# Query expansion in 32x64 tiles, numerators of all heads in one bank, and kv formed without a turn

One Trainium2 chip, one core. The metric is the device time of one execution in microseconds (us); lower is better. "Filled stretch" means the time from 25 us to about 255 us, in which TensorE never waits; "the head" is what comes before it. A turn is a transpose on TensorE, and a dummy is a product of zeros that only keeps TensorE busy.

## The reference

Attention with sketched features, then a feed-forward block with exact gelu:

```python
# q, k, v: (4 batches, 4 heads, 1088 tokens, 32);  S1, S2: (8, 32)
def phi(x):                                   # 64 features from two factors of 8
    a = einsum('rd,bhsd->bhsr', S1, x); b = einsum('rd,bhsd->bhsr', S2, x)
    return outer(a, b)                        # i, j -> 64
q_p, k_p = phi(q), phi(k)
kv  = einsum('bhsf,bhsd->bhfd', k_p, v)       # 64 x 32 per head
z   = k_p.sum(tokens)                         # 64 per head
x   = (q_p @ kv) / (q_p @ z + 1e-6)           # -> (4352, 128)
out = gelu(x @ w_in) @ w_out                  # w_in 128 x 2048, w_out 2048 x 128
```

The products are in fp32. The sketches and the feed-forward weights arrive in 64 bits and are first rounded to fp32 in steps named low words, fields, exponents, mantissas and signs. Each matrix product in the kernel is run by TensorE as two passes, each with its own weight load; the counts in the profile are passes (the 4 products of an expansion stand as x8).

## The kernel before: what the change and the argument touch

Heads are h = 2c + r: pair c, parity r. F = 64 features, D = 32, J = 8 blocks of 128 tokens; the 64 tokens a batch that are left are the rest tokens. `lhsT` is the stationary operand (the weight), `rhs` the moving one. A product takes a tile of the array, given as rows x columns; a change to another shape is a change of mode. I take it that the partitions of the output pick the column tile; the starts in the traces below bear this out (pairs 7 ns apart with outputs at two places, 58 ns apart at one).

```python
def kv_product(ps, lhsT, rhs, h, at, start=False):      # kv^T: v is the weight (32 columns)
    r = h % 2
    pe.matmul(ps[at * D:(at + 1) * D, r * F:(r + 1) * F], lhsT=lhsT, rhs=rhs, start=start, stop=False, ...)

def kv_first(ps, r):                                    # batch 0; v_aug = v | ones, 64 columns
    for i in range(J):
        ch, t, one = i // 4, i // 2 % 2, i % 2
        for c in range(NP):
            pe.matmul(ps[c * F:(c + 1) * F, r * F:(r + 1) * F], lhsT=v_aug[r][:, c, i, :],
                      rhs=k_p[0, r][:, t, c * 4 + ch * 2 + one].rearrange("p i j -> p (i j)"), ...)

def kv_sum(b, ps):                                      # batches 1 to 3
    for i in range(J):
        for h in range(H):
            kv_product(ps, main["v", b][:, h, i, :], k_p[b, h % 2][...], h, h, start=i == 0)
    # [cut] column sums of the features against ones, for z

def turn_kv(b, ps, copy):                               # kv^T -> kv, then the copy that attention reads
    # [cut] one transpose (b == 0) or two products with the identity
    copy(out=kz[b].rearrange("p c n -> p (c n)"), in_=ps[:, :128])

def expand_products(n):                                 # both factors of q: 4 products, 32 x 128 tiles
    for g in range(4):
        rows = slice(g * D, (g + 1) * D)
        pe.matmul(B_of[n][g // 2][:, g % 2, :W], lhsT=Srep[rows]..., rhs=qT[n][rows]..., start=True, stop=True)

def attend(n, ...):                                     # 4 products, 64 x 64 tiles, one bank per parity
    for c in range(NP):
        for r in range(2):
            pe.matmul(banks[r][c * F:(c + 1) * F, c0:c1], lhsT=kz[b][r * F:(r + 1) * F, c, :],
                      rhs=qp[n][r * F:(r + 1) * F, c, c0:c1], start=True, stop=True)
    # [cut] 4 copies of denominators on ScalarE, reciprocal, 4 multiplications on VectorE
```

## Time and profile before

| | before |
|---|---|
| time, median | 272.4 us (272.14 to 272.43) |
| span of the profiled run | 270.3 us |
| TensorE busy, share of the chain of waits | 98%, 95% |
| VectorE / ScalarE / GpSimd busy | 62% / 54% / 63% |
| first hidden product starts | 16.53 us |

The lines stand in the prediction below. One view of before that it leaves out is needed later: the chain in order of time (start us, duration us, engine, line, passes), where the first batch's kv is formed:

```profile
8.69 1.08 PE o_ps L414 x32
...
10.13 1.08 PE o_ps L414 x32
11.21 0.38 PE o_ps L434 x8
```

32 passes take 1.08 us, twice (L414), and the rest tokens 0.38 (L434).

### The profile page before, as it was taken

To read this page: it belongs to the slowest core of one execution; us is meant where nothing else is said; L and a number is where in the kernel's file an instruction comes from. 1 tells how busy PE (TensorE), PEld (TensorE's weight loads), DVE (VectorE), ACT (ScalarE), POOL (GpSimd) and SP (SyncE) were. 2 spreads that over 40 slices of the span, in tenths; PEclk is the share of its full clock that TensorE was granted. 3 is DMA by queue.
4 is the path that set the end of the run, shared out by engine and by line. 5 is a ranking of instruction groups with operands and counts; after the bars stand their busy time and mean duration, and the time that the engine had idled before them with its cause. 6 is when DMAs were issued, how large, how long until landed. Compare 5 with 4: busy or idle time off the path is not lost.

```text
span 270.3 us, 5814 instructions
## 1 busy us (share of the span) xinstructions
PE 264.2 (98%) x2320; PEld 135.7 (50%) x2320; DVE 167.4 (62%) x263; ACT 145.8 (54%) x291; POOL 171.5 (63%) x178
## 2 busy tenths in 40 slices
PE   7999999999999999999999999999999999999994
PEld 5735445354445545435445445444544544445794
DVE  6896888534795699679225997487048902750140
ACT  4784777566645633673367433763367334733431
POOL 3431007899998499368865897568856886777300
PEclk9999999999999999999999999999999999999999
DMA  6569263635201100110200000100200020011020
GB/s 198 171 172 359 54 170 65 171 75 143 53 2 21 21 0 2 21 22 0 42 0 2 0 0 12 32 0 4 38 0 2 1 39 4 1 22 19 2 39 20
DMA packets 37915, 13.50 MB, mean 50 GB/s; under 512 B 28288, under 2 KB 37248, under 8 KB 37888
## 3 DMA queue, kind: packets, MB, share of 16 engines
q1 hardware_dynamic: 37648, 13.05, 19.2%
q8 instruction: 18, 0.29, 0.5%
q10 hardware_dynamic: 240, 0.08, 0.1%
q14 instruction: 9, 0.07, 0.1%
HBM read 10.90 MB, written 2.23 MB: 49 GB/s over the span
## 4 chain that ended last, share of the span: by engine, by line
PE 95%; DVE 2%; DMA 1%; issue 0%; ACT 0%; ACTq 0%; DVEq 0%
PE h_ps L576 44%; PE o_ps L653 32%; PE o_ps L704 5%; PE w_ps L471 3%; PE w_ps L701 3%; PE w_ps L516 2%; PE w_ps L405 1%; PE w_ps L354 1%; DMA raw_SR<-in_S_dram 1%; PE o_ps L414 1%; PE h_ps L542 0%; PE w_ps L434 0%; DVE bits_m L272 0%; PE w_ps L542 0%; PE o_ps L310 0%
## 5 line engine op out<-in xcount | busy, mean ns | idle before, releaser
L576 PE MATMUL h_ps<-xT,w_in 128*64 128x512 f32 (+3 forms) x518 | 140.8, 577 | 0.2 <-DVE xT L561 0.2
L583 ACT ACTIVATE block<-h_ps 128x512 f32<-128x512 f32 (+1 forms) x128 | 72.8, 570 | 95.5 <-PE h_ps L576 93.1
L653 PE MATMUL o_ps<-block,w_out 128*64 128x256 f32 x224 | 57.8, 380 | 0.0
L576 PEld LDWEIGHTS h_ps<-xT,w_in 128*64 128x64 f32 (+1 forms) x518 | 42.1, 143 | 30.3 <-issue 10.1
L618 POOL TENSOR_TENSOR bits_low<-block 128x512 f32<-128x512 f32 x28 | 36.6, 1308 | 25.9 <-ACT block L583 25.7
L653 PEld LDWEIGHTS o_ps<-block,w_out 128*64 128x64 f32 x224 | 30.0, 137 | 38.4 <-issue 29.6
L619 POOL TENSOR_TENSOR bits_a<-block 128x512 f32<-128x512 f32 x28 | 36.9, 1316 | 16.2 <-ACT block L583 16.1
L492 DVE TENSOR_TENSOR q_pT<-A_sb,w_ps 64x512 f32<-64x512 f32 x32 | 22.1, 690 | 32.6 <-ACT A_sb L478 31.9
L621 POOL TENSOR_TENSOR bits_m<-block,bits_e 128x512 f32<-128x512 f32 x28 | 36.3, 1295 | 2.2
L620 POOL TENSOR_TENSOR bits_e<-bits_a,block 128x512 f32<-128x512 f32 x28 | 36.1, 1290 | 2.2
L524 DVE RECIPROCAL den<-den 128x512 f32<-128x512 f32 (+1 forms) x7 | 21.9, 3122 | 12.6 <-ACT den L523 12.6
L653 PE MATMUL o_ps<-bits_a,small 128*64 128x256 f32 x112 | 29.0, 382 | 0.0
L653 PE MATMUL o_ps<-bits_m,w_out 128*64 128x256 f32 x112 | 28.7, 379 | 0.0
L653 PE MATMUL o_ps<-block,small 128*64 128x256 f32 x112 | 28.7, 379 | 0.0
L653 PE MATMUL o_ps<-bits_low,small 128*64 128x256 f32 x112 | 28.7, 379 | 0.0
L653 PEld LDWEIGHTS o_ps<-block,small 128*64 128x64 f32 x112 | 15.3, 137 | 18.0 <-issue 12.8
L669 DVE TENSOR_TENSOR sums<-o_ps,sums 64x512 f32<-64x512 f32 x8 | 5.5, 682 | 24.6 <-ACT sums L666 24.6
L478 ACT COPY A_sb<-w_ps 64x512 f32<-64x512 f32 (+1 forms) x36 | 17.7, 557 | 3.9 <-PE w_ps L471 3.8
L528 DVE TENSOR_TENSOR xT<-w_ps,den 32x512 f32<-32x512 f32 (+1 forms) x28 | 18.2, 648 | 1.0
L653 PE MATMUL o_ps<-bits_e,small 128*64 128x256 f32 x112 | 16.8, 379 | 0.0
L704 PE MATMUL o_ps<-g,w_out 128*128 128x512 f32 x32 | 16.4, 599 | 0.3 <-ACT xT L561 0.3
L523 ACT ACTIVATE den<-w_ps 32x512 f32<-32x512 f32 (+1 forms) x28 | 15.6, 558 | 1.3 <-PE w_ps L516 1.0
(158 smaller groups left out, 320.4 us busy)
## 6 DMA issues: line engine op xcount, KB each, us to landing
block<-in_moe_w_in_dram SPq DMA_DIRECT2D x3, 512.0 KB, 7.2
block<-in_moe_w_out_dram SPq DMA_DIRECT2D x3, 512.0 KB, 9.9
k<-in_k_dram SPq DMA_DIRECT2D x48, 32.0 KB, 1.9
v<-in_v_dram SPq DMA_DIRECT2D x3, 512.0 KB, 4.2
q<-in_q_dram SPq DMA_DIRECT2D x24, 64.0 KB, 3.6
out_dram<-oT SPq DMA_DIRECT2D x24, 64.0 KB, 2.2
k<-in_k_dram SPq DMA_DIRECT2D x2, 256.0 KB, 3.1
q<-in_q_dram SPq DMA_DIRECT2D x2, 256.0 KB, 4.2
```

Source lines behind the costliest of these rows:

```text
L478: act.copy(out=A[g // 2][F:, g % 2, :width[n]], in_=B_of[n][g // 2][:F, g % 2, :width[n]])
L492: dve.tensor_mul(out=cols[r * F:(r + 1) * F], in0=a[:, :, r::2], in1=b[:, :, r::2])
L524: dve.reciprocal(out=den[:, :W], in_=den[:, :W])
L528: dve.tensor_mul(out=xT[n][rows, :W], in0=banks[h % 2][rows, :W], in1=den[rows, :W])
L576: pe.matmul(ps[rows, :W], lhsT=w[:, rows], rhs=xT[n][:, :W], start=True, stop=True)
L583: act.activation(out=g_of[n, fi][:, :W], in_=ps[:, :W], func=ACT.Gelu)
L618: pool.tensor_sub(out=s[3], in0=a11, in1=a21)
L619: pool.tensor_add(out=s[1], in0=a21, in1=a22)
L620: pool.tensor_sub(out=s[2], in0=s[1], in1=a11)
L621: pool.tensor_sub(out=s[4], in0=a12, in1=s[2])
L653: pe.matmul(acc[n][bank][half * 64:(half + 1) * 64, col:col + HW], lhsT=fixed, rhs=moving, start=opens and e == 0 and name in "4715", stop ...
L704: pe.matmul(o_of[n], lhsT=w_tile(w_out_sb, fi), rhs=g, start=first, stop=final)
```

## The change

Three parts. (1) kv is formed directly: the features become the weight, v moves, so no turn is needed. (2) The query expansion puts both factors of a head on the same partitions: 16 products in 32x64 tiles in place of 4 in 32x128; half the copies and multiplications follow. (3) The attention puts the numerators of all heads in one bank: 8 products in 64x32 tiles, then one multiplication. Also two small dummy products in the head, one older dummy ahead of the token attention dropped, and some rounding of weights moved between engines there. The zeros of the dummies shrink to one column, so that the first warm-up product starts at 0.93 us and not at 1.20.

```diff
-    def kv_product(ps, lhsT, rhs, h, at, start=False):
-        r = h % 2
-        pe.matmul(ps[at * D:(at + 1) * D, r * F:(r + 1) * F], lhsT=lhsT, rhs=rhs, start=start, ...)
+    def kv_product(ps, features, rhs, h, at, start=False):
+        c, r = h // 2, h % 2
+        pe.matmul(ps[r * F:(r + 1) * F, c * 2 * D + at:c * 2 * D + at + rhs.shape[1]],
+                  lhsT=features..., rhs=rhs, start=start and c == 0, ...)
     def kv_first(ps, r):
         for i in range(J):
             for c in range(NP):
-                pe.matmul(ps[c * F:(c + 1) * F, r * F:(r + 1) * F], lhsT=v_aug[r][:, c, i, :], rhs=k_p[0, r][...], ...)
+                kv_product(ps, k_p[0, r][...], v_aug[r][:, c, i, :], 2 * c + r, 0, start=i == 0)
     def kv_sum(b, ps):
-                kv_product(ps, main["v", b][:, h, i, :], k_p[b, h % 2][...], h, h, start=i == 0)
+                kv_product(ps, k_p[b, h % 2][...], main["v", b][:, h, i, :], h, h % 2 * D, start=i == 0)
-    def turn_kv(b, ps, copy):   [cut]
     def expand_products(n):
-        for g in range(4):
-            pe.matmul(B_of[n][g // 2][:, g % 2, :W], lhsT=Srep[rows]..., rhs=qT[n][rows]..., ...)
+        for s in range(2):
+            for g in range(G):
+                for r in range(2):
+                    pe.matmul(B_of[n][g // 2][r * F:(r + 1) * F, g % 2, s * W // 2:(s + 1) * W // 2],
+                              lhsT=Srep[rows, s]..., rhs=qT[n][rows, r::2]..., ...)
     def attend(n, ...):
-                    pe.matmul(banks[r][c * F:(c + 1) * F, c0:c1], lhsT=kz[b][r * F:(r + 1) * F, c, :], ...)
+                    for part, ps in ((r, over), (1 - r, under)):
+                        pe.matmul(ps[c * F + part * D:c * F + (part + 1) * D, c0:c1],
+                                  lhsT=kz[b][r * F:(r + 1) * F, c, part * D:(part + 1) * D], ...)
-        for h in range(H):
-            dve.tensor_mul(out=xT[n][rows, :W], in0=banks[h % 2][rows, :W], in1=den[rows, :W])
+        dve.tensor_mul(out=xT[n][:, :W], in0=over[:, :W], in1=den[:, :W])
-    key_turn(0, 1, hidden_bank(), by_act, midway=sketches)
+    key_turn(0, 1, hidden_bank(), by_act, midway=lambda: (keep_busy(1, bank, 128), sketches()))
+    keep_busy(1, bank, 64)
```

(Cut: the copies and multiplications of the expansion, the rest tokens' kv, the order of the roundings.)

More of the change, by code (lines that the diff above doesn't have):

```diff
@@ L226 @@
     pad_v_rem(0)
-    idle = big.tile([128, 256], FP, name="idle")
+    idle = big.tile([128, 1], FP, name="idle")
     dve.memset(idle, 0.0)
@@ L316, in four_tokens @@
         return main[n, b][:, h, c * JC:(c + 1) * JC, :].rearrange("p j d -> p (j d)")
-    kT, k_p, k_p_rem, kv_T = {}, {}, {}, {}
+    kT, k_p, k_p_rem = {}, {}, {}
     def widen_v(r):
@@ L400, in add_tokens @@
         eng.tensor_add(out=k_s[r][:, :, 0], in0=k_s[r][:, :, 0], in1=k_s[r][:, :, 1])
-    def kv_product(ps, lhsT, rhs, h, at, start=False):
-        r = h % 2
-        pe.matmul(ps[at * D:(at + 1) * D, r * F:(r + 1) * F], lhsT=lhsT, rhs=rhs, start=start, stop=False,
-                  skip_group_check=True)
+    def kv_product(ps, features, rhs, h, at, start=False):
+        c, r = h // 2, h % 2
+        pe.matmul(ps[r * F:(r + 1) * F, c * 2 * D + at:c * 2 * D + at + rhs.shape[1]],
+                  lhsT=features.rearrange("p i j -> p (i j)") if len(features.shape) == 3 else features, rhs=rhs,
+                  start=start and c == 0, stop=False, skip_group_check=True)
     def kv_first(ps, r):
@@ L413, in kv_first @@
             for c in range(NP):
-                pe.matmul(ps[c * F:(c + 1) * F, r * F:(r + 1) * F], lhsT=v_aug[r][:, c, i, :],
-                          rhs=k_p[0, r][:, t, c * 4 + ch * 2 + one].rearrange("p i j -> p (i j)"),
-                          start=(r == 0 and i == 0), stop=False, skip_group_check=True)
+                kv_product(ps, k_p[0, r][:, t, c * 4 + ch * 2 + one], v_aug[r][:, c, i, :], 2 * c + r, 0, start=i == 0)
     def kv_sum(b, ps):
@@ L422, in kv_sum, with take_kv @@
             for h in range(H):
-                kv_product(ps, main["v", b][:, h, i, :],
-                           k_p[b, h % 2][:, t, h // 2 * 4 + ch * 2 + one].rearrange("p i j -> p (i j)"),
-                           h, h, start=i == 0)
+                kv_product(ps, k_p[b, h % 2][:, t, h // 2 * 4 + ch * 2 + one], main["v", b][:, h, i, :], h, h % 2 * D,
+                           start=i == 0)
         for m in range(2):
             for h in range(H):
-                c, r = h // 2, h % 2
-                kv_product(ps, ones, k_s[r][:, c, 0, m], h, 2 * c + 1 - r)
+                kv_product(ps, k_s[h % 2][:, h // 2, 0, m], ones, h, (1 - h % 2) * D)
     def kv_sum_rem(b, ps):
-        for r in range(2):
-            for c in range(NP):
-                pe.matmul(ps[c * F:(c + 1) * F, r * F:(r + 1) * F], lhsT=v_rem_aug[b][:, 2 * c + r, :],
-                          rhs=k_p_rem[b % 2][:, 2 * c + r].rearrange("p i j -> p (i j)"),
-                          start=False, stop=True, skip_group_check=True)
-    def take_kv(b, ps, copy):
-        kv_T[b] = att.tile([128, 128], FP, name="kv_T")
-        copy(out=kv_T[b], in_=ps[:, :128])
-    def turn_kv(b, ps, copy):
-        if b == 0:
-            pe.transpose(ps[:, :128], in_=kv_T[b], identity=ident)
-        else:
-            for rows in (slice(0, 64), slice(64, 128)):
-                pe.matmul(ps[rows, :128], lhsT=kv_T[b][:, rows], rhs=ident, start=True, stop=True)
-        copy(out=kz[b].rearrange("p c n -> p (c n)"), in_=ps[:, :128])
+        for h in range(H):
+            kv_product(ps, k_p_rem[b % 2][:, h], v_rem_aug[b][:, h, :], h, 0)
+    def take_kv(b, ps):
+        act.copy(out=kz[b].rearrange("p c n -> p (c n)"), in_=ps[:, :128])
     qT, qp, xT = {}, {}, {}
@@ L467, in expand_products @@
         W = width[n]
-        B_of[n] = [work_banks() for g in range(2)]
-        for g in range(4):
-            rows = slice(g * D, (g + 1) * D)
-            pe.matmul(B_of[n][g // 2][:, g % 2, :W], lhsT=Srep[rows].rearrange("p a i j -> p (a i j)"),
-                      rhs=qT[n][rows].rearrange("p h j t -> p (h j t)"), start=True, stop=True)
+        B_of[n] = [work_banks() for i in range(2)]
+        for s in range(2):
+            for g in range(G):
+                for r in range(2):
+                    rows = slice(g * D, (g + 1) * D)
+                    pe.matmul(B_of[n][g // 2][r * F:(r + 1) * F, g % 2, s * W // 2:(s + 1) * W // 2],
+                              lhsT=Srep[rows, s].rearrange("p i j -> p (i j)"),
+                              rhs=qT[n][rows, r::2].rearrange("p c j t -> p c (j t)"), start=True, stop=True)
@@ L473, in expand_products, with expand_copy @@
         qp[n] = att.tile([128, NP, CW], FP, name="q_pT")
-    def expand_copy(n, g):
-        if g % 2 == 0:
-            A[g // 2] = att.tile([128, 2, CW], FP, name="A_sb", bufs=2)
-        act.copy(out=A[g // 2][F:, g % 2, :width[n]], in_=B_of[n][g // 2][:F, g % 2, :width[n]])
+    def expand_copy(n, i):
+        A[i] = att.tile([128, 2, CW // 2], FP, name="A_sb")
+        act.copy(out=A[i][:, :, :width[n] // 2], in_=B_of[n][i][:, :, :width[n] // 2])
     def expand_multiply(n, i):
         W = width[n]
-        a, b = (t[F:, :, :W].rearrange("f g (h x) -> f g h x", h=H) for t in (A[i], B_of[n][i]))
+        a, b = (t.rearrange("f g (c x) -> f g c x", c=NP) for t in (A[i][:, :, :W // 2], B_of[n][i][:, :, W // 2:W]))
@@ L484, in expand_multiply @@
         if n < NMAIN:
-            cols = qp[n].rearrange("f n (g x) -> f g n x", g=G)[:, 2 * i:2 * i + 2]
-        else:
-            cols = qp[n][:, :, :W].rearrange("f n (j g t) -> f g n j t", g=G, t=32)[:, 2 * i:2 * i + 2]
-            a, b = (x.rearrange("f g h (j t) -> f g h j t", t=32) for x in (a, b))
-        for r in range(2):
-            if n < NMAIN:
-                dve.tensor_mul(out=cols[r * F:(r + 1) * F], in0=a[:, :, r::2], in1=b[:, :, r::2])
-            else:
-                for g in range(2):
-                    dve.tensor_mul(out=cols[r * F:(r + 1) * F, g], in0=a[:, g, r::2], in1=b[:, g, r::2])
+            dve.tensor_mul(out=qp[n].rearrange("f c (g x) -> f g c x", g=G)[:, 2 * i:2 * i + 2], in0=a, in1=b)
@@ L497, in query_features @@
+            return
+        cols = qp[n][:, :, :W].rearrange("f c (j g t) -> f g c j t", g=G, t=32)
+        a, b = (x.rearrange("f g c (j t) -> f g c j t", t=32) for x in (a, b))
+        for g in range(2):
+            dve.tensor_mul(out=cols[:, 2 * i + g], in0=a[:, g], in1=b[:, g])
     def query_features(n, i):
-        for g in range(2):
-            expand_copy(n, 2 * i + g)
+        expand_copy(n, i)
         expand_multiply(n, i)
@@ L511, in attend @@
         owners = [(0, W, n // NCH)] if n < NMAIN else [(i * REM, (i + 1) * REM, i % 2 * 2 + i // 2) for i in range(B)]
-        banks = halves(work_banks())
+        over, under = halves(work_banks())
         for (c0, c1, b) in owners:
@@ L515, in attend @@
                 for r in range(2):
-                    pe.matmul(banks[r][c * F:(c + 1) * F, c0:c1], lhsT=kz[b][r * F:(r + 1) * F, c, :],
-                              rhs=qp[n][r * F:(r + 1) * F, c, c0:c1], start=True, stop=True)
+                    for part, ps in ((r, over), (1 - r, under)):
+                        pe.matmul(ps[c * F + part * D:c * F + (part + 1) * D, c0:c1],
+                                  lhsT=kz[b][r * F:(r + 1) * F, c, part * D:(part + 1) * D],
+                                  rhs=qp[n][r * F:(r + 1) * F, c, c0:c1], start=True, stop=True)
         meanwhile()
@@ L522, in attend @@
             at = c * F + (1 - r) * D
-            act.activation(out=den[h * D:(h + 1) * D, :W], in_=banks[r][at:at + D, :W], func=ACT.Copy, bias=1e-6)
+            act.activation(out=den[h * D:(h + 1) * D, :W], in_=under[at:at + D, :W], func=ACT.Copy, bias=1e-6)
         dve.reciprocal(out=den[:, :W], in_=den[:, :W])
         xT[n] = att.tile([128, CW], FP, name="xT", bufs=3)
-        for h in range(H):
-            rows = slice(h * D, (h + 1) * D)
-            dve.tensor_mul(out=xT[n][rows, :W], in0=banks[h % 2][rows, :W], in1=den[rows, :W])
+        dve.tensor_mul(out=xT[n][:, :W], in0=over[:, :W], in1=den[:, :W])
     x_tok = {}
@@ L733, in keep_busy @@
         for i in range(n):
-            pe.matmul(ps[:, CW - cols:], lhsT=idle[:, 0:128], rhs=idle[:, :cols], start=True, stop=True)
+            pe.matmul(ps[:, CW - cols:], lhsT=idle.broadcast_to([128, 128]), rhs=idle.broadcast_to([128, cols]),
+                      start=True, stop=True)
     bank = work_bank()
@@ L753 @@
     key_turn_rem(0, banks[1], by_dve)
-    for g in range(2):
-        expand_copy(0, g)
-    expand_multiply(0, 0)
+    for i in range(2):
+        query_features(0, i)
     kv_bank = out_bank()
     kv_first(kv_bank, 0)
-    expand_copy(0, 2)
     key_features_rem(0, banks[1], by_pool=True)
-    expand_copy(0, 3)
-    expand_multiply(0, 1)
     load_w_out(0, gated=True)
@@ L769 @@
     w_in[0].fields()
-    take_kv(0, kv_bank, by_act)
+    w_in[1].low_words()
     late = []
     query_turn(1, lambda **a: late.append(a))
-    turn_kv(0, kv_bank, by_act)
-    w_in[1].low_words()
+    take_kv(0, kv_bank)
     w_in[0].exponents()
     by_act(**late[0])
+    w_in[0].mantissas()
     w_in[1].fields()
     w_in[0].signs()
-    w_in[0].mantissas(by_pool=True)
+    w_in[0].product(pool)
     load_rest()
     w_out.append(Rounding(w_out_sb[1], beside=w_in[1]))
-    w_in[0].product(pool)
     w_in[1].exponents()
     banks = [hidden_bank(), hidden_bank()]
-    keep_busy(1, banks[0], 128)
     attend_by_token(0, banks)
@@ L793 @@
     w_in[1].product(pool)
-    for g in range(1, 4):
-        expand_copy(1, g)
-    expand_multiply(1, 0)
+    expand_copy(1, 1)
+    for i in range(2):
+        expand_multiply(1, i)
     w_out[0].fields()
-    expand_multiply(1, 1)
     steps = [(n, fi) for f in range(0, USUAL, 4) for n in range(NCH) for fi in range(f, f + 4)]
@@ L846, in finish_keys @@
         kv_sum_rem(b, held["kv"])
-        take_kv(b, held["kv"], by_act)
+        take_kv(b, held["kv"])
     def round_at(t, w, product_by=dve):
@@ L874 @@
     at(21, finish_keys, 1)
-    at(22, lambda: turn_kv(1, held["kv"], by_act))
     at(23, query_turn, 3)
@@ L896 @@
             at(t + 16, finish_keys, b)
-            at(t + 17, lambda b=b: turn_kv(b, held["kv"], by_act))
     products = {t: [] for t in range(len(steps) + LAG)}
```

## The prediction

> **What bounds the kernel now.** I read the page first: is an engine full, and does the chain that ended last run through it?
>
> ```profile
> span 270.3 us, 5814 instructions
> PE 264.2 (98%) x2320; PEld 135.7 (50%) x2320; DVE 167.4 (62%) x263; ACT 145.8 (54%) x291; POOL 171.5 (63%) x178
> PE 95%; DVE 2%; DMA 1%; issue 0%; ACT 0%; ACTq 0%; DVEq 0%
> ```
>
> TensorE is both the busiest engine (98%) and 95% of the chain of waits; DVE and ACT are little over half busy. Then the waits of TensorE alone, whole:
>
> ```profile
> PE w_ps L734 <- DVE idle L228: 1.2, 1, 1.2
> PE w_ps L296 <- DVE SR L282: 0.3, 1, 0.3
> PE h_ps L558 <- DVE x_tok L550: 0.3, 1, 0.3
> PE o_ps L704 <- ACT xT L561: 0.3, 1, 0.3
> PE h_ps L576 <- DVE xT L561: 0.2, 1, 0.2
> ```
>
> All five fall before 25 us. Then the busy time by stretches: from 50 to 250 us TensorE is busy 200.0 of 200 us. So there are two regimes. From 25 us on, work taken off DVE or ACT is worth nothing, and only time on TensorE counts. Before 25 us there is a chain of dependent steps, where a step removed may count. The chain in order of time, in the head:
>
> ```profile
> 11.59 0.58 PE o_ps L310 x4
> 12.18 0.12 PE o_ps L444
> 12.30 0.02 issue
> 12.33 0.27 ACT kz L448
> 12.60 0.04 issue
> 12.64 1.21 PE h_ps L542 x64
> ...
> 15.15 0.86 DVE bits_m L272
> 16.00 0.39 DVE xT L561
> 16.39 0.14 issue
> 16.53 3.87 PE h_ps L576 x8
> ```
>
> The turn of kv (L444), its copy and the token attention (L542) follow one another; the first hidden products (L576) start at 16.53. And the same chain around a key stage of the filled stretch:
>
> ```profile
> 104.66 1.25 PE w_ps L405 x80
> 105.91 0.38 PE w_ps L434 x8
> ...
> 108.02 0.22 PE w_ps L447 x4
> ...
> 109.96 1.07 PE w_ps L471 x8
> ...
> 115.91 1.02 PE w_ps L516 x8
> ```
>
> kv sum 1.25 + 0.38, its turn 0.22, a query expansion 1.07, an attention 1.02. These blocks are what the change touches. (A matrix product in the text is two passes, each with its own weight load.)
>
> **What the skill says.** (1) The Trainium skill, "TensorE: Matmul & The Clock Gate", section "LDWEIGHTS (loading the stationary operand)": a load's time goes with its columns (columns / 1.2 ns), not its rows. The trace agrees: weight loads take 110, 137 and 190 ns for 32, 64 and 128 columns, so 27 and 53 ns for 32 and 64 more. (2) The same page, Part 3, "The mechanism": products in different tiles of the array run together, a few ns apart. The trace agrees: the four 32*128 products of L471 start at 71.596, .603, .609 and .616, that is 7 ns apart, and eight passes of 512 columns take 1.07 us where single ones follow at 0.43. (3) "TensorEngine Tiling (Array Packing)", "Key Properties": a change of tiling mode drains the engine. The trace agrees in size: L405 starts 0.10 us after the pace of the products before it would have it. (4) "PSUM — Partial Sum Buffer", "PSUM bank collisions raise a hardware error": two row tiles must not write one bank in the same quadrant. No run shows this yet; I checked the change by hand below.
>
> **The change, part by part.**
>
> kv without a turn. Removed: the turn (0.22 us each for b = 1, 2, 3; 0.12 in the head) and an ACT copy. But the operands change places: before, v is the weight (32 columns, four column tiles) and the key features move (64 columns); after, the features are the weight (64 columns, two column tiles) and v moves (32). What is the pace? Before, 64 passes start from 104.59 to 105.50: 14.2 ns a pass, 57 ns a tile. L414 has 64 weight columns in two tiles: successive products of one tile start 58 ns apart, 29 ns a pass. L354 settles what bounds it: there 64 weight columns meet only 32 moving ones, and still a tile takes 58 ns from start to start. So the load of 64 columns sets 58 ns however little moves. With two tiles in place of four, the 80 passes take 80 x 29 = 2.34 us, and the 8 of the rest 0.23: 2.57 us. Before: 1.63, mode change included (the new form keeps the 128*64 mode of its neighbours, so that has no change to add). That is +0.94, less the turn 0.22: +0.72, three times: **+2.2 us**, all on the path. For b = 0 the kv products have 64 by 64 before and after: no difference.
>
> Query expansion. Before 4 products of 128 weight columns and 512 moving ones in four tiles; after 16 of 64 and 256 in eight tiles. Each tile now has 4 passes of 256 columns (0.213) in place of 2 of 512 (0.427): 0.854 us either way. The first load of a tile is exposed: 0.107 becomes 0.053; the stagger of eight starts costs 4 x 7 ns more. Net -0.02 us, on 8.5 stages: **-0.2 us**. Row group g writes only bank g: no clash. On ACT 4 copies of 0.56 become 2 of about 0.59, and on DVE 4 products of 0.69 become 2 of the same length (same elements per partition): -1.0 and -1.4 us a chunk, beside other work from 25 us on.
>
> Attention. Before 4 products in 64*64, after 8 in 64*32, all in different tiles: 0.854 + load + start either way, with 4 more starts and a load of 32 in place of 64 columns: about **0**. Each quadrant gets row half 0 in one bank and row half 1 in the other, so no clash. DVE has 1 product of 128 partitions for 4 of 32: -1.9 us, hidden.
>
> The head. From the end of the query turns (12.18) the token attention can start, since the kv copy, now straight from the sum, runs from 11.64 to 11.91 where the copy for the turn stood, beside those turns; and the query features are ready at 10.6 rather than 12.43. So it starts near 12.15 in place of 12.64: -0.5. DVE's mantissas (L272, 0.86 us in the chain, its like elsewhere 0.42, with POOL busy beside it) give some 0.2 back, as POOL now does the other product earlier. The first hidden products take 3.87 us where 8 passes of 0.43 take 3.44: ACT still has three expansion copies (16.14 to 17.69) ahead of the gelu that frees the bank. One copy of 0.59 there leaves no such wait: -0.4. The two small dummy products added stand in gaps (4.9 to 5.4 us, 5.9 to 6.1) and may cost 0.1. Sum: **-1.0 us** by 25 us.
>
> Total: 272.4 + 2.2 - 0.2 - 1.0 = **273.4 us**.
>
> **The rivals.** (a) Eight tiles don't run together as four do (no block here uses eight): each expansion and attention would take up to 0.85 us more, 8.5 + 6.5 stages, +12 us, to 285. Against: the four-tile blocks start at 7 ns steps, 32 passes at 7 ns are 0.22 us, far under 0.85; and the skill's page tells of sixteen at once. For: nothing here has shown it. If only the attention, now with both row halves in each bank, suffers: +5.5, to 279. (b) The kv products run at the pace of issue (14 ns a pass) since loads overlap better than in L354: then kv costs 1.3 + 0.2 instead of 2.57 and the turn is pure gain: 271.2 or a little under. Against: L354's 58 ns. (c) The head's gain is lost on the way: the next link after the hidden products is the rounding of the output weights on DVE (last write 21.35, its reader at 21.41), and if it doesn't move up, only 0.3 to 0.5 of the 1.0 stays: 274.0. For moving up: DVE has 1.4 us less of expansion before it. (d) Relief of ACT and DVE speeds the filled stretch, by several us. Against: TensorE has no wait there to take away.
>
> **Range and chances.** Between (b), 271.2, and (c), 274.0, lies nearly all; the kv term could be off by 0.5 and the head by 0.4. I take 271.6 to 274.7. 2% is 5.4 us: faster by that would need (d), 0.01. Slower by it needs (a), 0.04. Within: 0.95.
>
> **What would show it.** Right: kv blocks of x80 near 2.3 to 2.4 us in the chain and no turn; expansion blocks of x32 near 1.05; attention x16 near 1.0; TensorE still 98% busy; the stretch of 25 to 250 us longer by some 2 us for the same work; first hidden product near 15.8, and hidden products of the head in 3.44. Wrong: an x80 block at 1.25 (rival b), an expansion or attention of 1.5 to 2 us (rival a), a hidden start after 16.2 (c), or a total under 270 or over 276.

## The result, and the profile after

276.04 us median (275.67 to 276.22, four runs) against 272.38 for the kernel before: ratio 1.0135, 95% interval 1.0117 to 1.0152. It is slower, within the 2% to which the prediction gave 0.95, but outside its range of 271.6 to 274.7. A ratio here is the mean time of one kernel's fast runs over that of the other's of the same rounds, so it isn't quite the ratio of the medians quoted.

The page of the changed kernel, the lines that answer to the first ones of the prediction:

```profile
span 274.2 us, 6306 instructions
PE 268.8 (98%) x2605; PEld 143.3 (52%) x2605; DVE 139.2 (51%) x223; ACT 136.0 (50%) x268; POOL 170.8 (62%) x177
PE 96%; DMA 1%; DVE 1%; issue 0%; SPq 0%
```

VectorE lost 28 us of work and ScalarE 10, and yet the span grew by 3.9: relief of these engines did not show, as expected. TensorE's own time grew. The chain in order of time, filled stretch (kv sum, expansion, attention):

```profile
106.84 2.56 PE w_ps L406 x88
...
112.85 1.05 PE w_ps L460 x32
...
118.78 1.02 PE w_ps L501 x16
```

These three blocks are as predicted: 2.57, about 1.05, about 1.0. The same chain in the head:

```profile
5.56 0.43 PE w_ps L718 x2
5.98 0.21 PE w_ps L296
6.20 0.37 PE h_ps L310 x2
6.57 0.17 PE w_ps L718 x2
6.74 0.60 PE o_ps L354 x32
...
9.22 2.01 PE o_ps L406 x32
...
11.60 2.24 PE o_ps L406 x40
13.84 0.59 PE o_ps L310 x4
14.43 1.14 PE h_ps L526 x64
...
18.24 3.83 PE h_ps L560 x8
```

This is not as predicted. The first batch's kv (L406) takes 2.01 and 2.24 us where L414 and L434 took 1.08 and 1.08 + 0.38, and both dummies (L718) stand on the chain. From the two chains, the lag of the changed kernel behind the one before grows so:

| at the start of | before | after | lag | step |
|---|---|---|---|---|
| first key product | 6.12 | 6.74 | 0.62 | +0.62 |
| first batch's kv | 8.69 | 9.22 | 0.53 | -0.09 |
| query turns (kv done) | 11.59 | 13.84 | 2.25 | +1.72 |
| token attention | 12.64 | 14.43 | 1.79 | -0.46 |
| first hidden product | 16.53 | 18.24 | 1.71 | -0.08 |
| second block of hidden products | 25.22 | 26.64 | 1.42 | -0.29 |
| last chunk's projection (by its first start) | 255.16 | 258.98 | 3.82 | +2.40 |

So there are two losses of like size: about 2.4 us in the filled stretch, foreseen as 2.0, and 1.4 in the head, where a gain of 1.0 was foreseen.

### The profile page after: what moved, and what is told of

The parts are those of the page before. It is cut to its first block, busy times and chain, and to the rows that moved or that the text cites. A ratio compares the mean times of both kernels' runs of the same rounds, so it can differ in the third digit from the quotient of the medians.

```text
span 274.2 us, 6306 instructions
## 1 busy us (share of the span) xinstructions
PE 268.8 (98%) x2605; PEld 143.3 (52%) x2605; DVE 139.2 (51%) x223; ACT 136.0 (50%) x268; POOL 170.8 (62%) x177
## 4 chain that ended last, share of the span: by engine, by line
PE 96%; DMA 1%; DVE 1%; issue 0%; SPq 0%
PE h_ps L560 43%; PE o_ps L637 31%; PE o_ps L688 5%; PE w_ps L460 3%; PE w_ps L406 3%; PE w_ps L685 3%; PE w_ps L501 3%; PE o_ps L406 2%; DMA k<-in_k_dram 1%; PE w_ps L354 1%; PE h_ps L526 0%; PE w_ps L526 0%; PE h_ps L310 0%; PE o_ps L310 0%; DVE x_tok L534 0%; PE h_ps L542 0%
## 5 line engine op out<-in xcount | busy, mean ns | idle before, releaser
L473 DVE TENSOR_TENSOR q_pT<-A_sb,w_ps 128x512 f32<-128x512 f32 x16 | 10.3, 682 | 40.2 <-ACT A_sb L467 40.2
L637 PEld LDWEIGHTS o_ps<-bits_low,small 128*64 128x64 f32 x112 | 15.3, 137 | 0.0
L637 PEld LDWEIGHTS o_ps<-bits_m,w_out 128*64 128x64 f32 x112 | 15.2, 137 | 0.0
```

The lines of the kernel that those rows point to most:

```text
L473: dve.tensor_mul(out=qp[n].rearrange("f c (g x) -> f g c x", g=G)[:, 2 * i:2 * i + 2], in0=a, in1=b)
L637: pe.matmul(acc[n][bank][half * 64:(half + 1) * 64, col:col + HW], lhsT=fixed, rhs=moving, start=opens and e == 0 and name in "4715", stop ...
```

## The experiments

My theory after this: in `kv_first` the old form sent successive products (c = 0, 1) to two column tiles, since the output stood at partitions c * F. The new form puts the output at r * F, and r is fixed within a call, so all 32 passes of a call queue in one tile. The trace has the starts: in the old form pairs 7 ns apart, one pair every 58 ns; in the new form single starts every 58 ns. Rivals: the exchange of operands is slow in itself, the dummies, the eight-tile blocks or the mode changes they bring.

### Alternate the column tiles in the new form

```diff
-    def kv_first(ps, r):
+    def kv_first(ps):
         for i in range(J):
-            for c in range(NP):
+            for c, r in ((c, r) for c in range(NP) for r in range(2)):
-    kv_first(kv_bank, 0)
     key_features_rem(0, banks[1], by_pool=True)
     load_w_out(0, gated=True)
-    kv_first(kv_bank, 1)
+    kv_first(kv_bank)
```

> The changed kernel, but the first batch's kv products of both head parities are issued in one interleaved loop, so that successive products fall in different column tiles; same 64 passes, same operands. Theory (in the changed kernel each call of the first kv sum keeps to one column tile, so its passes follow at 58 ns instead of 29): the two blocks of 2.01 and about 1.9 us become one of about 1.9, starting later, at some 10.0 us, since it waits for both feature tiles; total 276.0 - 1.7 = 274.3 us. Rival (features as weights are slow in themselves, or the DMA and clock set the head): no change or up to 0.8 us more, 276 to 276.8.

Measured: 274.36 us median (six runs, one of them 276.33), ratio 1.0084 (1.0061 to 1.0108). The chain of waits in its head:

```profile
9.83 2.25 PE o_ps L406 x72
12.08 0.59 PE o_ps L310 x4
12.67 1.14 PE h_ps L526 x64
```

All 72 passes of the first batch's kv take 2.25 us where 72 took 4.25 in the changed kernel. The same operands in the same number of passes, only dealt to two tiles in turn, give back 1.7 us by the medians. In the two profiles 0.42 of it is an earlier start of the keys (first key product at 6.32 and not 6.74 us); from there to the end of kv it is 5.76 us for 7.10, that is 1.34 less. It isn't all of the loss: the one block starts later, at 9.83 for 9.22, since it waits for both feature tiles.

### The reverse: one tile at a time in the kernel before

```diff
-        for i in range(J):
+        for c, i in ((c, i) for c in range(NP) for i in range(J)):
             ch, t, one = i // 4, i // 2 % 2, i % 2
-            for c in range(NP):
-                pe.matmul(ps[c * F:(c + 1) * F, ...
+            pe.matmul(ps[c * F:(c + 1) * F, ...
```

> The kernel before, with only the order of the first batch's kv products turned: all of one head pair, then all of the other, so that successive products fall in the same column tile. Operands, sizes and number as before. Theory (alternation of column tiles is what the change lost there): each block of 32 passes goes from 1.08 to 2.0 us, total 272.4 + 1.85 = 274.2 us. Rival (the exchange of weight and moving operand, or the place of the output, made the changed kernel's blocks slow): within 0.2 us of 272.4.

Measured: 273.69 us (22 runs), ratio 1.0045 (1.0023 to 1.0067): slower by about 1.3, not by 1.85. Its chain:

```profile
8.66 1.83 PE o_ps L414 x32
...
10.85 1.65 PE o_ps L414 x29
```

The direction settles it: order alone makes the old form slow too (from the first key product to the end of kv 6.82 us for 5.47, 1.35 more), so the exchange of operands is not needed for the loss here. The size fell short because a call here has one crossing from one tile to the other, and there the trace shows the passes of both in pairs again (starts at 9.338 and 9.344, 9.451 and 9.455, 9.509 and 9.513 us), and the rest tokens' products ran beside the end of the second block. Outside the crossing the starts are 58 ns apart.

### No dummies

```diff
-    key_turn(0, 1, ..., midway=lambda: (keep_busy(1, bank, 128), sketches()))
-    keep_busy(1, bank, 64)
+    key_turn(0, 1, ..., midway=sketches)
```

> The changed kernel without the two added dummy products in the head. Theory (both stand on the chain, 0.43 and 0.17 us at half clock): 276.0 - 0.6 = 275.4 us, first key product some 0.6 us earlier. Rival (they stand in gaps that the loads of the keys and the sketches leave, as the prediction had it): within 0.15 us of 276.0; if they keep the clock up, without them it is slower by some tenths.

Measured: 275.41 us (275.27 to 275.77, four runs), ratio 1.0113 (1.0098 to 1.0128): 0.6 us less than the changed kernel's median, as the theory had it. The two intervals overlap, and the moment at which TensorE's clock rises differs from run to run, so from these times alone the size is good to some tenths only. More profiles help: by the timelines the first key products start at 6.26 to 6.78 us in the five of this study that have the dummies and at 5.76 to 6.06 in the four fast ones with the same warm-up and no dummies, 0.6 us between the means.

### The kv part alone put back

```diff
-    [kv_product, kv_first, kv_sum, kv_sum_rem, take_kv as changed]
+    [the same and turn_kv as before, called where they were]
```

> The changed kernel with the kv part alone put back as before (v as weights, the turn, its copies); query expansion, attention and dummies as changed. Theory (kv is the whole loss: 3 x 0.71 us in the filled stretch and 0.93 + 0.78 in the head, less 0.46 for the turn on the head's chain): 276.0 - 2.1 - 1.25 = 272.6 us, near the kernel before. Rival (eight tiles, new mode changes or the dummies make the loss): it stays over 274.5.

Measured: 272.68 us (22 runs, 272.06 to 273.2), ratio 1.0002 (0.9986 to 1.0018). The edit also puts the head's order back, the copy of kv ahead of the second rounding. kv is the whole net loss: all the rest of the change together lies between -0.4 and +0.5 us, with 27.6 us less VectorE work in all (139.8 for 167.4). That is a balance and not a row of zeros: the dummies and the attention have costs, and smaller gains stand against them (the sum is below).

### What sets the pace of the kv sums: load or moving columns

In batches 1 to 3, 64 columns of v move in place of 32 against the same 64 weight columns (results wrong on purpose, and the run says so):

```diff
-    kv_product(ps, k_p[...], main["v", b][:, h, i, :], h, h % 2 * D, start=i == 0)
+    kv_product(ps, k_p[...], main["v", b][:, h, i // 2 * 2:i // 2 * 2 + 2, :]..., h, 0, start=i == 0)
```

> The changed kernel, but in the kv sums of batches 1 to 3 each product moves 64 columns (v of two tokens) in place of 32, with the same 64 weight columns; results wrong on purpose. Theory (the weight load of 64 columns sets 58 ns per product of a tile, and 64 moving columns take no longer than that): the blocks of 88 passes stay at 2.56 us and the total within 0.2 us of 276.0. Rival (what moves sets the pace, or load and moving add up): 27 ns more per product of a tile, 64 passes in two tiles, +0.85 us a batch, 278.6 us.

Measured: 275.72 us, ratio 1.0108 (1.0058 to 1.0158). The kv block in its chain:

```profile
106.96 2.56 PE w_ps L406 x88
```

It has the same 2.56 us to the digit; the median of its four runs lies 0.3 below the changed kernel's, where I had expected 0.2 at most. Doubling what moves costs nothing. What is left to set the pace of the changed kernel's kv sums is the 64-column load, or a fixed cost per pass, which the next run tests.

### Split the load: 32 weight columns in four tiles

```diff
-                kv_product(ps, k_p[...], main["v", b][:, h, i, :], h, h % 2 * D, start=i == 0)
+                for half in range(2):        # lhsT = features[:, half * D:(half + 1) * D]
+                    kv_half(ps, k_p[...], main["v", b][:, h, i, :], h, h % 2 * D, half, start=i == 0)
# [cut] kv_half itself; the column sums are split in the same way
```

> The changed kernel, but in the kv sums of batches 1 to 3 each product is split in two with 32 weight columns each, in four column tiles; 160 passes in place of 80, still no turn. Theory (the load of 64 columns, 58 ns a tile, sets the pace; a load of 32 columns takes half): 8 ns a pass, 160 x 8 = 1.28 us and the rest about 0.4 with its mode changes, 1.7 in place of 2.56, total 276.0 - 2.5 = 273.5 us. Rival (a fixed cost of some 58 ns per product of a tile, or 29 ns per pass whatever the tile): 2.3 us or more for the 160, total 275.3 or slower than 276.

Measured: 274.66 us (274.1 to 275.27), ratio 1.0083 (1.0068 to 1.0098), 1.4 faster than the changed kernel and not 2.5. The block of the sum and that of the rest tokens in its chain:

```profile
106.18 1.49 PE w_ps L413 x98
107.67 0.38 PE w_ps L406 x8
```

1.87 us in place of 2.56. Twice the passes in less time, so the rival of a fixed cost per pass is out. But by starts in the trace the 160 passes take 1.49 us in two batches, 9.3 ns each and not 8, and 1.81 in the third, with two pauses of 0.10 and 0.14 us whose cause wasn't looked for; and the change to 128*32 tiles comes back: some 0.1 us before each of the three blocks. The old form with its turn, 1.25 + 0.38 + 0.22 = 1.85, is as cheap.

### Put together what won

First batch's kv in the new form on two tiles, batches 1 to 3 in the old form with the turn, no dummies. Its edit is the first and third diff above, with `kv_sum` and `turn_kv` of before for b > 0.

> The changed kernel with the first batch's kv in the new form but alternating between the column tiles, batches 1 to 3 in the form of before with the turn, and without the two dummy products. Theory (the parts add up): the kernel with kv undone came to 1.0002 of before, less 0.6 for the dummies, less 0.2 for the first batch's turn: 271.6 us, ratio 0.997. Rival (the dummies' cost is regained by a clock that rises earlier, and the wait for both feature tiles takes the rest): 272.2 to 272.6.

Measured: 272.45 us (14 runs), ratio 0.9994 (0.9968 to 1.0021); the rival's figure, not mine. The same with the attention of before (its 4 products and 4 multiplications):

> The same with the attention put back into 64 by 64 tiles in two banks (4 products in place of 8, 4 multiplications on DVE in place of 1). Theory (in the filled stretch only TensorE's time counts: the attentions took 6.52 us in the kernel before and 6.90 in the changed one, and the key products after two of them another 0.1 for the mode change): 0.45 us faster than the run before it, 271.2 us, in spite of 1.9 us more DVE work a chunk. Rival (the relief of DVE is worth something): slower than the run before it.

Measured: 272.49 us (22 runs), ratio 1.0 (0.9979 to 1.0021), no faster. One thing that stood in the way is in the timeline of ScalarE of the second of them (start us, us, operation, [idle before it]):

```profile
12.55 0.43 ACT L252 ACTIVATE bits_low<-small 128x256 f32<-128x256 uint32 x1 [2.39 <-DMA small<-in_moe_w_in_dram]
12.89 0.25 ACT L434 COPY kz<-o_ps 128x128 f32<-128x128 f32 x1
```

The sum that the kv copy reads was ready before 12 us, but ScalarE stood 2.39 us at the rounding of the second input weights, whose load had not landed. The change had moved that rounding ahead of the copy; in the changed kernel itself kv came so late that it did no harm. The clock is another matter. The profile of the first of the two fell on a slow run (276.4 us; the ratios leave its two slow runs out), and its chain reads:

```profile
8.36 1.94 PE w_ps L499 x32
...
11.78 4.04 PE o_ps L406 x72
```

The expansion takes 1.94 us where it takes 1.05 elsewhere, and 72 passes take 4.04 where the first experiment has 2.25: TensorE ran at half clock, by the trace's record until 16.5 us. In the other profiles the clock rose between 3.8 and 7.0 us. The kernel before has such times too, 275 to 276 in 6 of 51 runs; whether they are the same event isn't shown, as only this one was profiled.

So the copy was put back ahead of the rounding, with either attention:

```diff
-    w_in[1].low_words()
     late = []
     query_turn(1, lambda **a: late.append(a))
     take_kv(0, kv_bank)
+    w_in[1].low_words()
```

> The run with the old attention, but ScalarE takes the copy of kv ahead of the low words of the second input weights, as the kernel before did. Theory (in that run the kv copy stood behind low words whose load landed at 12.47 us, and that took the gain of the head): token attention at some 12.6 us in place of 13.19, 0.55 us faster, 271.9 us in the fast runs; the next limit is the load of the second queries, which the query turns wait for. Rival (the DMA order is as late for whatever comes next): within 0.2 us of 272.5. Some runs in which the TensorE clock rises late may show 4 us more.

Measured: 271.61 us (22 runs, one of them slow at 275.61), ratio 0.9973 (0.9955 to 0.9991). Token attention starts at 12.63 us in place of 13.19: 0.56 of the 0.9 by which the median fell is the wait taken away, as expected; the rest isn't explained. It is the best kernel of the study, by 0.3%, which is little.

> The same with the changed attention (eight 64 by 32 tiles, one bank for the numerators). Theory: the attention costs 0.45 us more on TensorE and its relief of DVE is worth nothing, 272.3 us. Rival: equal or faster than the run before it.

Measured: 272.05 us (14 runs), ratio 1.0005 (0.9988 to 1.0021): by the medians the changed attention costs 0.44 us, as expected from the trace. Runs of 273 to 274 in both make the intervals overlap, so the time alone wouldn't prove it; the blocks do. Summed from each block's first start to the next block's, the attentions of the filled stretch take 6.90 us with eight tiles and 6.52 with four. Of the 0.38, 0.16 lies in the last chunk, with 64 passes in place of 32 (0.79 and 0.63 us), and 0.22 in the two attentions that key products follow (1.02 and 0.91 us each). Those key products have 64*64 tiles, as the old attention had, and now bear a change of mode that it spared them. The chain puts the whole of it to their account, 0.16 us each; kernel before:

```profile
86.82 0.90 PE w_ps L354 x64
```

and changed kernel, same view:

```profile
88.84 1.06 PE w_ps L354 x64
```

## Why the prediction was wrong

**The step that failed.** "For b = 0 the kv products have 64 by 64 before and after: no difference." The sizes are indeed the same; what I didn't follow through is where the outputs stand. The new output place makes a whole call of `kv_first` fall in one column tile, at 58 ns a pass in place of 29. I had used the alternation of tiles in the later batches' sums and took it for granted here. In place of 0 it cost 1.72 us. Giving the alternation back (1.7 us by the medians, 1.34 in the trace) and taking it from the kernel before (1.3 us) both show it.

**The dummies.** "May cost 0.1": they stand on the chain with 0.43 and 0.17 us, and leaving them out gave 0.6. I had read the gaps from one profile in which the sketch's load was late and the clock rose at 4.6 us, and read them too wide: TensorE is idle there from 5.08 to 5.41 and from 6.01 to 6.12 us. In the profile after, the clock rose at 6.2 us and the sketches were ready earlier, so the dummies ran at half speed with nothing to hide behind.

**The rest of the head.** The turn off the chain, -0.5: measured -0.46, right. The mantissas, -0.2: the step from the end of x_tok to the first hidden product is 1.38 before and 1.37 after, so nothing; the transposes of x_tok, which ran beside the mantissas before, fill it. The hidden products' wait for ScalarE, -0.4: the block went from 3.87 to 3.83. The copies ahead of the gelu were not what held it. ScalarE is idle 1.07 us before the first gelu in the changed kernel, and the block is as long; that the product, its gelu and the next use of the bank are the loop is my reading, not tested. Some 0.3 came later, up to 26.6 us, which I hadn't placed.

**The filled stretch.** kv +2.2: the blocks came to 2.56 for 2.57, and 7.69 us for three batches from start to start against 5.25 before, less some 0.3 of mode changes that ended before the old block: 2.1. Right, and its reason, the load, holds with twice the moving columns. Expansion -0.2: 6.29 for 6.42 and 0.62 for 0.64 us, -0.15, and all eight tiles start 7 ns apart: right. Attention 0: +0.38, and +0.1 at the key products behind it. Four of the six full chunks take 1.02 us before and after, as predicted; I left out that the last chunk's many short passes double in number (0.16), and that the key products behind two attentions now come after another mode (0.16 each by the chain, the attention's part of it included).

**The rivals.** (a), eight tiles not running together, and (b), the sums at the pace of issue, are out. (The figure for (b), 271.2, had left the head's 1.0 out; by the prediction's own terms it is some 270.2, so the range was too narrow at its lower end. And 80 x 29 is 2.32; 2.34 is with 29.2 ns.) (c), the head's gain lost on the way, happened for another reason. (d), relief of the other engines, was worth nothing: with kv put back, 27.6 us less VectorE work leaves the time at a ratio of 1.0002.

The sum from the measured terms: kv of batches 1 to 3 2.1, of batch 0 1.72 - 0.46, dummies 0.6, attention and key products 0.5, expansion -0.15, other head -0.4: 3.9, the growth of the span.

## What to carry to other kernels

When operands of a small product change places, write down for each loop which tile of the array each successive product falls in: here the output's partitions decided it, and the same products ran at half the pace when they queued in one tile (58 ns a pass for 29). Count tiles before you weigh loads: in the sums of batches 1 to 3 a tile took 56 to 58 ns a pass in both forms, and the old one was twice as fast because its 32 weight columns left room for four tiles in place of two. With 64 weight columns the load set that pace, whether 32 or 64 moved; so here the narrower operand belonged in the array, even at the price of the turn. Where one engine is full, count only that engine's time; and in the head of a kernel, look at what each queue puts ahead of the copy on the chain.

## What the Trainium skill lacked or had wrong

- "TensorE: Matmul & The Clock Gate", "LDWEIGHTS (loading the stationary operand)", gives the length of a load, and the section before it spacings for 128 and 512 moving columns, but nothing gives the pace of products with narrow weights that follow each other in one tile. Here it was 58 ns for 64 weight columns, with 32 or with 64 moving ones (2.56 us for 88 passes in two tiles either way).
- The same page, Part 3, "The mechanism", gives about 4 ns between the starts of products in different tiles; here it was 7 ns in the blocks with four or eight tiles of both kernels (with the sums split to 32 by 32 columns the steps were uneven, 0 to 17 ns). Eight 32*64 tiles at once worked as it says: 32 passes of 256 columns in 1.05 us.
- "TensorEngine Tiling (Array Packing)", "Key Properties", says that a mode change drains the array, with no figure. Here a change cost some 0.1 to 0.16 us on the way in (L354 0.90 us after a block of its own mode, 1.06 after another).
- The same first page, "What's actually happening", puts the rise of the clock at about 3.4 us of sustained work. Here, with the first product at 0.93 to 1.20 us, it rose 3.8 to 7.0 us after the span's start, and in one run at 16.5 us with TensorE busy 3.89 of the first 5 us; that run was 4 us longer.
